# Top-k attention and Fourier mixing on one core: the scores of two query tiles in one burst of four matmuls, the second tile's fetched from the banks of the transposes one and two steps later

## The chip, the cores and the metric

The kernel runs on one core of a Trainium2 chip. The metric is the device time of one execution in microseconds (us). TensorE is called PE in the profile, VectorE DVE, ScalarE ACT, GpSimd POOL; SP issues DMAs.

## What is computed

```python
def _attn_ref(q, k, v):                      # (8, 8, 576, 64): batch, heads, tokens, head size
    scores = scale * np.matmul(q, k.transpose(0, 1, 3, 2))
    kth = np.partition(scores, -top_k, axis=-1)[..., -top_k:-top_k + 1]      # top_k = 32
    scores = np.where(scores >= kth, scores, -1000000000.0)
    attn = np.exp(scores - np.max(scores, axis=-1, keepdims=True))
    attn = attn / (np.sum(attn, axis=-1, keepdims=True) + 1e-09)
    return np.matmul(attn, v)
# attention's output as x (8, 576, 512), then
    X = np.fft.fft(np.fft.fft(x, axis=1), axis=2)
    u = x + np.real(X)
    un = (u - mean(u)) / np.sqrt(var(u) + 1e-06)
    return u + np.maximum(un @ w_ch1, 0.0) @ w_ch2      # 512 -> 2048 -> 512
```

All arithmetic is in 32-bit floats. The weights come as 64-bit floats and are converted in the first stage.

## The kernel before

Heads are worked on in pairs, four pairs to a batch and 32 in all. The 64 columns of one head lie on partitions 0 to 63 and those of the other on 64 to 127, so that the two heads' score matmuls use different halves of PE's rows. A pair's queries make five tiles: four of 128 rows, each of which gives two items (one per head), and one of 64 rows in which both heads lie together. In the order of `IN_PAIR` a pair has nine items: tile 0 (items 0 and 1), tile 1 (2, 3), the small tile 4 (item 4), tile 2 (5, 6), tile 3 (7, 8). There are 288 items, and one step of the main loop for each.

Everything is written out in one hand-made order. Step i does the following, each engine taking its instructions strictly in this order:

- PE computes scores for item j = i + 3. For an item with head 0 the function `scores` makes two matmuls of 128 x 512 (L401), one for each head, whose results ACT copies into the tiles `S` (L404). The last 64 keys, called the tails, come from a matmul of their own (`sp_t`, L371) and are copied by two short copies (L375). The small tile has its own form (L386, L393).
- DVE finds the 32 largest of 576 scores in four rounds of `max` (L425) and three of `match_replace` (L427): the last two rounds of item i and the first two of item i + 1.
- POOL then makes the two bounds `nt` (L434). In the next step ACT writes a mask into `wk` (L448), POOL subtracts it (L451), and ACT takes the exponential (L459).
- In most pairs (pairs 4, 5, 6 and 8 to 30: `by_dma`) the probabilities are transposed by DMA: ACT splits each 32-bit word into two planes (two copies, L472), SP writes them to DRAM (L485 and L488) and reads them back transposed (`turn`, L506) into `PT`. In the others PE transposes them (L527).
- PE multiplies `PT` by v (`o`, L564), ACT copies the result (`xT`, L578) and the sums (`rd`, L590), PE transposes it back to tokens (`tpx`, L604), and DVE normalises it into x (L608, L615).
- At steps 0 and 5 of a pair PE transposes the next q and k (`prep`, L308).

Beside the attention of one batch run the transforms and the two-layer network of an earlier one. The Fourier transform is folded on POOL (`fold_ops`, L651 to L719), multiplied on PE (`yp`, L755; `mp`, L812 and L816) and copied by ACT (`y`, L786 to L791; `us`, L833); POOL adds it to x (L839), DVE takes the statistics (L844). The network is cut into units: `hidden` (hp, L966, with ACT's copy hT, L970) and `back` (cp, L993 and L1032; the products cv and cw, L1163, with sums on POOL, L1108, copies on ACT, L1133, and loads of `w2` parts on SP, L909). A planner decides how many units a step takes: `fixed_cost` is its estimate of the step's other PE work, `level` the common height to which steps are filled, and `some` runs units after each piece of the step's PE list `fixed`. The list begins with the scores; work in `last_scores` is put at its end, and there stood the scores of a pair's tile 0.

PSUM has eight banks: two for scores (`ps_s`), two for the transposes of q, k and probabilities and, in `by_dma` pairs, for the tails (`ps_t`), one for o and tpx (`ps_o`), three for the units (`ps_m`). Buffers of a pool are handed out in turn; a matmul into a bank waits until ACT has read what was there before. `S` has six buffers, `W` (the tiles `wk`) three.

Of the kernel before, what the change touches and what calls it, by code (L numbers as in the profile page):

```python
# [9 lines left out]
F32 = mybir.dt.float32  # L10
# [9 lines left out]
P = 128  # L20
# [53 lines left out]
def kernel(  # L74
# [9 lines left out]
    nc = tc.nc  # L84
    B, H, S, D = q.shape
# [5 lines left out]
    NF = NC - 1  # L91
# [239 lines left out]
    items = [(pair, t, e) for pair in range(NPAIR) for t, e in IN_PAIR]  # L331
    N = len(items)

    def scores(i, part):


# [3 lines left out]
        pair, t, e = items[i]  # L340
        qT, kT = qT_of[pair], kT_of[pair]
        rows = ROWS[t]
        if part == 0:
            for n in range(1 if e is None else 2):
                Ssb[i + n] = attp.tile([P, S], F32, name=f"S_{i + n}", tag="S", bufs=6)
        q_cols = slice(P * t, P * t + rows)
# [91 lines left out]
    def pair_by_dma(pair):  # L438

        return NPB <= pair < NPAIR - 1 and pair != 2 * NPB - 1  # L440

    def by_dma(i):
        return pair_by_dma(i // PER_PAIR)
# [22 lines left out]
    def plane(i, half):  # L466

        if not (0 <= i < N and by_dma(i)):
            return
        words = Wk[i].bitcast(U16).rearrange("p (h s) -> p h s", h=2)  # L470
        src = Ssb[i].bitcast(U16).rearrange("p (s h) -> p h s", h=2)
        nc.scalar.copy(out=words[:, half, :], in_=src[:, half, :])  # L472
        if half == 0:
            return
        Ssb.pop(i)
        Wk.pop(i)
        pair, t, e = items[i]
        nq = TAIL if e is None else P
        if e != 1:
            planes_of[pair, t] = dramp.tile(  # L480
                [nq, 2, 2 * S], U16, name=f"planes_{pair}_{t}", tag="planes", bufs=3
            )
        to = planes_of[pair, t]
        if e is not None:
            nc.sync.dma_start(out=to[:, :, S * e:S * (e + 1)], in_=words)  # L485
        else:
            for h in range(2):
                nc.sync.dma_start(  # L488
                    out=to[:, :, S * h:S * (h + 1)], in_=words[nq * h:nq * (h + 1)]
                )  # L490
        if e != 1:
            Wp.pop(i)
# [965 lines left out]
    def fixed_cost(i):  # L1458

        t = 0.55 if 0 <= i - 2 < N and not by_dma(i - 2) else 0.0  # L1460
        if i + 3 < N:
            t += {0: 1.04, 1: 0.3, None: 0.9}[items[i + 3][2]]
            if by_dma(i + 3) and items[i + 3][2] is not None:
                t += -0.3 if items[i + 3][2] else 0.3
        ch = chunk_at(i)[1] if i > PER_BATCH + 3 else {4: 0, 8: 1}.get((i - 3) % PER_PAIR)
        t += 0.0 if ch is None else (CW[ch] / 115.0 + 0.14 * len(CHUNKS[ch]))
        if i < N and i % PER_PAIR in (0, 5):
            t += 0.7
        return t + costs.get(i, 0.0)
# [9 lines left out]
    def run(i, where):  # L1479
        for fn in plan.pop((i, where), []):  # L1480
            fn()
# [16 lines left out]
    while i < N + 5 or plan or queue or sums:  # L1498
# [18 lines left out]
        if i < N and i % PER_PAIR == 5:  # L1517
            preps.append(lambda: prep("k", pair_of + 1))
        last_scores = []
        if PER_BATCH < j < N and j % PER_PAIR == 0 and by_dma(j):  # L1520
            fixed.append(lambda: 0.0)
            last_scores.append(lambda: scores(j, 0) + scores(j, 1))
        elif e == 0 and by_dma(j):
            fixed.append(lambda: scores(j, 0) + scores(j, 1))
        elif e != 1:
            fixed.append(lambda: scores(j, 0))
        elif not by_dma(j):
            fixed.append(lambda: scores(j - 1, 1))
        else:
            fixed.append(lambda: 0.0)  # L1530
# [13 lines left out]
            fixed += tok  # L1544
        for where in ("pe1", "pe2", "pe"):
            fixed += plan.pop((i, where), [])
        if e is None and j < N:
            fixed.append(lambda: scores(j, 1))
        n_tr = len(fixed)
        if done is not None:  # L1550
# [19 lines left out]
            mask(i - 1)  # L1570
        plane(i - 2, 0)
        plane(i - 2, 1)
        run(i, "convert")
        if short:
            expo(i - 1)
# [98 lines left out]
```

## Time and profile before

| | |
|---|---|
| median of three runs | 1861.7 us (1857.86 to 1864.14) |
| profiled execution, its own time | 1856.28 us |
| span in the profile | 1854.5 us |
| mean granted PE clock | 0.96 |
| busy PE / DVE / ACT / POOL | 1688.5 / 1584.3 / 1294.3 / 912.5 us |
| score matmuls L401 | 528 records, 170.4 us busy |
| fetches of scores L404 | 264 copies, 588 ns mean |
| tails sp_t L371 | 320 records |

One matmul of 32-bit floats appears as two records, each with its own weight load (PEld). A row of the timeline merges equal instructions that follow each other: start, length of the merged run, engine, line, operation, tiles written and read, size, count, and in brackets the idle time before it and the instruction that ended it. The profile shows one execution, and durations are taken from there; so a sum is made against 1856.28 us.

### The profile page before, as it was taken

What the parts mean: (1) busy time and instruction counts of PE and PEld (TensorE: products, weight loads), DVE (VectorE), ACT (ScalarE), POOL (GpSimd) and SP (SyncE); (2) the same over time, 40 slices, a digit from 0 to 9 for tenths busy, and PEclk for the clock granted to TensorE, in tenths of its full rate; (3) what the DMA queues carried; (4) which work ended last, traced back from release to release, by engine and by line L of the source; (5) the groups of instructions that cost most, each with busy time, mean ns of one, the idle gap of its engine ahead of it and who ended that gap; (6) DMA issues with size and microseconds to landing.
All of it is one profiled execution on the core that took longest, in us unless ns stands there. A gap on an engine that the chain in (4) does not pass through costs nothing.

```text
span 1854.5 us, 26992 instructions
## 1 busy us (share of the span) xinstructions
PE 1688.5 (91%) x8134; PEld 1082.4 (58%) x8134; DVE 1584.3 (85%) x3301; ACT 1294.3 (70%) x3104; POOL 912.5 (49%) x1278
## 2 busy tenths in 40 slices
PE   5676699789899898999999999999999999999999
PEld 3343465355465664557565665667565756686677
DVE  7999989889999999999999999999999998944010
ACT  6878658577688778878788778877887778642100
POOL 4768743454753466346543565355634654350012
PEclk8778799899999999999999999999999999999999
DMA  5333115661456954568465945586457845520051
GB/s 168 106 88 114 27 41 148 186 168 38 121 137 158 233 151 123 134 178 222 112 153 146 246 124 137 141 222 171 122 137 180 213 112 140 153 82 7 6 173 57
DMA packets 516576, 249.16 MB, mean 134 GB/s; under 512 B 398288, under 2 KB 506448, under 8 KB 516432
## 3 DMA queue, kind: packets, MB, share of 16 engines
q1 hardware_dynamic: 515664, 247.23, 51.2%
q8 instruction: 65, 1.06, 0.2%
q14 instruction: 79, 0.65, 0.1%
q10 hardware_dynamic: 768, 0.21, 0.0%
HBM read 93.63 MB, written 84.74 MB: 96 GB/s over the span
## 4 chain that ended last, share of the span: by engine, by line
PE 43%; DVE 24%; POOL 11%; ACT 9%; issue 7%; DMA 4%; SPq 1%; POOLq 0%; DVEq 0%; ACTq 0%
PE hp L966 15%; DVE wk L427 11%; DVE m L425 10%; PE o L564 5%; PE cp L993 5%; POOL wk L451 5%; PE cw L1163 4%; PE sp L401 3%; ACT wk L448 2%; PE cv L1163 2%; POOL fg L651 2%; PE yp L755 2%; ACT wk L472 1%; POOL zw L678 1%; PE cp L1032 1%
## 5 line engine op out<-in xcount | busy, mean ns | idle before, releaser
L451 POOL TENSOR_TENSOR wk<-S,wk 128x576 f32<-128x576 f32 x288 | 407.5, 1415 | 485.2 <-ACT wk L448 484.8
L425 DVE MAX8 m<-wk 128x8 f32<-128x576 f32 x864 | 626.4, 749 | 6.1
L966 PE MATMUL hp<-unT,w 128*128 128x256 f32 (+1 forms) x2048 | 526.1, 409 | 5.3 <-ACT hT L970 4.6
L966 PEld LDWEIGHTS hp<-unT,w 128*128 128x128 f32 x2048 | 380.3, 191 | 109.8 <-issue 10.4
L427 DVE MATCH_REPLACE8 wk<-m,wk 128x576 f32<-128x576 f32 x576 | 427.5, 742 | 0.0
L472 ACT COPY wk<-S 128x576 uint16<-128x576 uint16 x468 | 289.6, 670 | 0.0
L448 ACT ACTIVATE wk<-S,nt 128x576 f32<-128x576 f32 x288 | 223.4, 776 | 85.3 <-POOL nt L434 84.0
L993 PE MATMUL cp<-w,hT 128*128 128x512 f32 x512 | 234.9, 599 | 0.0
L970 ACT ACTIVATE hT<-hp 128x320 f32<-128x320 f32 (+1 forms) x256 | 103.3, 411 | 177.2 <-PE hp L966 175.6
L425 DVE MAX8 m<-S 128x8 f32<-128x576 f32 x288 | 213.7, 742 | 15.6 <-ACT S L375 15.6
L459 ACT ACTIVATE S<-wk,nt 128x576 f32<-128x576 f32 x234 | 184.2, 787 | 50.5 <-POOL wk L451 49.2
L427 DVE MATCH_REPLACE8 wk<-m,S 128x576 f32<-128x576 f32 x288 | 213.7, 742 | 0.0
L564 PE MATMUL o<-PT,v 128*64 128x256 f32 (+3 forms) x1440 | 199.3, 421 | 14.5 <-ACT x L627 5.9
L401 PE MATMUL sp<-kT,qT 64*128 64x512 f32 (+1 forms) x528 | 170.4, 673 | 12.2 <-ACT means L1357 5.7
L564 PEld LDWEIGHTS o<-PT,v 128*64 128x64 f32 x1440 | 115.7, 155 | 90.8 <-issue 22.3
L404 ACT COPY S<-sp 128x512 f32<-128x512 f32 (+1 forms) x264 | 141.8, 588 | 27.9 <-PE sp L401 26.9
L993 PEld LDWEIGHTS cp<-w,hT 128*128 128x128 f32 x512 | 93.9, 192 | 90.2 <-issue 89.3
L1108 POOL TENSOR_TENSOR hT<-hT 128x512 f32<-128x512 f32 x64 | 81.2, 1275 | 117.0 <-ACT hT L970 87.9
L434 POOL TENSOR_TENSOR nt<-m,cc 128x2 f32<-128x2 f32 x288 | 60.2, 209 | 155.4 <-DVE m L425 154.8
L1163 PE MATMUL cw<-w,hT 128*128 128x256 f32 x448 | 105.3, 385 | 12.2 <-ACT ct L1133 10.1
L371 PEld LDWEIGHTS sp_t<-kt,qT 128*128 128x128 f32 x320 | 51.0, 194 | 108.9 <-issue 67.6
L1163 PEld LDWEIGHTS cw<-w,hT 128*128 128x128 f32 x448 | 83.1, 191 | 27.9 <-ACT ct L1133 12.5
(160 smaller groups left out, 2129.6 us busy)
## 6 DMA issues: line engine op xcount, KB each, us to landing
planes<-wk SPq DMA_DIRECT2D x208, 288.0 KB, 2.7
w<-w_parts SPq DMA_DIRECT2D x82, 512.0 KB, 4.7
space<-in_moe_w_ch_dram SPq DMA_DIRECT2D x32, 512.0 KB, 3.6
nat<-in_q_dram SPq DMA_DIRECT2D x128, 64.0 KB, 2.3
v<-in_v_dram SPq DMA_DIRECT2D x64, 128.0 KB, 2.9
out_dram<-x SPq DMA_DIRECT2D x32, 256.0 KB, 2.8
nat<-in_k_dram SPq DMA_DIRECT2D x62, 128.0 KB, 3.0
planes<-wk SPq DMA_DIRECT2D x52, 144.0 KB, 2.6
```

What stands on the lines that cost most here:

```text
L401: nc.tensor.matmul(sp[r], lhsT=qT[hd, q_cols], rhs=kT[hd, :], start=True, stop=True)
L404: nc.scalar.copy(out=s_t[r, keys], in_=sp[r])
L425: ops.append(lambda src=src, m8=m8: nc.vector.max(out=m8, in_=src))
L427: ops.append(lambda src=src, m8=m8: nc.vector.match_replace(w, m8, src, NEG))
L448: nc.scalar.activation(out=w, in_=Ssb[i], func=AF.Relu, scale=-FAR, bias=Nt[i][:, 1:2])
L451: nc.gpsimd.tensor_tensor(out=w, in0=Ssb[i], in1=w, op=ALU.subtract)
L459: nc.scalar.activation(out=Ssb[i] if by_dma(i) else w, in_=w, func=AF.Exp, bias=Nt.pop(i)[:, 0:1], accum_out=den_t[pair % 3][:, c:c + 1],)
L472: nc.scalar.copy(out=words[:, half, :], in_=src[:, half, :])
L564: nc.tensor.matmul(o[D * e:D * (e + 1), c0:c1], lhsT=vv[:, c, e, :], rhs=pt[:, NF if c == NF else (NF + 1) * e + c, c0:c1], start=(c == 0) ...
L966: nc.tensor.matmul(hp[:, 0:w], lhsT=w1[:, dt, P * it:P * (it + 1)], rhs=unT[:, dt, 0:w], start=(dt == 0), stop=(dt == NDT - 1),)
L993: nc.tensor.matmul(cp, lhsT=hT[:, it, P * n:P * (n + 1)], rhs=w2[:, it, :], start=(it == 0), stop=(it == NIT - 1),)
L1163: nc.tensor.matmul(dst, lhsT=h()[a][:, kc, :], rhs=rhs_of(kc), start=start and kc == 0, stop=kc == NK - 1, skip_group_check=True,)
```

## The change

In the pairs with transposes by DMA, the scores of two tiles of 128 rows are computed in one burst of four matmuls: tiles 0 and 1 at the end of the step that used to do tile 0 (only where the pair before is such a pair too), tiles 2 and 3 at the end of the step that used to do tile 2 at its beginning. The first tile's two results go to the score banks and are copied at once, as before. The second tile's two results go to the two banks of `ps_t` and stay there; ACT copies them with `fetch`, head 0 one step later, head 1 two steps later, behind the plane copies of that step. The tails keep their steps, and there they now stand alone: before the burst for tiles 0 and 2, at the usual place for tiles 1 and 3. The planner's estimates follow: 2.4 us in a burst step, 0.3 us in the second tile's step.

```diff
+    def in_burst(i):
+        if not (0 <= i < N and by_dma(i)):
+            return False
+        r = i % PER_PAIR
+        return r >= 5 or (r < 4 and pair_by_dma(i // PER_PAIR - 1))
+
+    held = {}
+
+    def burst(i):
+        pair, t, _ = items[i]
+        for n, pool, tag in ((0, ps_s, "sp"), (2, ps_t, "tp")):
+            t = items[i + n][1]
+            for h in range(2):
+                hd = slice(D * h, D * (h + 1))
+                sp = pool.tile([P, NF * P], F32, name=f"sp_{i + n}_{h}", tag=tag)
+                nc.tensor.matmul(
+                    sp, lhsT=qT_of[pair][hd, P * t:P * (t + 1)], rhs=kT_of[pair][hd, :],
+                    start=True, stop=True,
+                )
+                held[i + n + h] = sp
+        for h in range(2):
+            fetch(i + h)
+        return 2.1
+
+    def fetch(i):
+        if i not in held:
+            return
+        if i not in Ssb:
+            Ssb[i] = attp.tile([P, S], F32, name=f"S_{i}", tag="S", bufs=6)
+        keys = slice(TAIL, S) if items[i][2] else slice(0, NF * P)
+        nc.scalar.copy(out=Ssb[i][:, keys], in_=held.pop(i))
...
-            if by_dma(i + 3) and items[i + 3][2] is not None:
+            if in_burst(i + 3):
+                t = t - 1.04 + {0: 2.4, 5: 2.4, 2: 0.3, 7: 0.3}[(i + 3) % PER_PAIR] if items[i + 3][2] == 0 else t - 0.3
+            elif by_dma(i + 3) and items[i + 3][2] is not None:
                 t += -0.3 if items[i + 3][2] else 0.3
...
-        if PER_BATCH < j < N and j % PER_PAIR == 0 and by_dma(j):
+        if in_burst(j) and e == 0:
+            fixed.append(lambda: scores(j, 1) if j % PER_PAIR else 0.0)
+            if j % PER_PAIR in (0, 5):
+                last_scores.append(lambda: burst(j))
+        elif PER_BATCH < j < N and j % PER_PAIR == 0 and by_dma(j):
             fixed.append(lambda: 0.0)
             last_scores.append(lambda: scores(j, 0) + scores(j, 1))
...
-        if e is None and j < N:
+        if j < N and (e is None or in_burst(j) and j % PER_PAIR == 0):
             fixed.append(lambda: scores(j, 1))
...
         plane(i - 2, 0)
         plane(i - 2, 1)
+        if j % PER_PAIR in (1, 2, 6, 7):
+            fetch(j + 1)
         run(i, "convert")
```

More of the change, by code (lines that the diff above doesn't have):

```diff
@@ L342, in scores @@
         rows = ROWS[t]
-        if part == 0:
+        if part == 0 or in_burst(i) and i not in Ssb:
             for n in range(1 if e is None else 2):
```

## Prediction

> **What bounds the kernel now.** I read the page first: part 1 and the chain of part 4.
>
> ```profile
> PE 1688.5 (91%) x8134; PEld 1082.4 (58%) x8134; DVE 1584.3 (85%) x3301; ACT 1294.3 (70%) x3104; POOL 912.5 (49%) x1278
> PE 43%; DVE 24%; POOL 11%; ACT 9%; issue 7%; DMA 4%; SPq 1%; POOLq 0%; DVEq 0%; ACTq 0%
> ```
>
> These are averages over stages, so I cut the span with the windows view (columns: stretch, length, busy time and instructions of PE, PEld, DVE, ACT, POOL, granted clock, DMA share, GB/s).
>
> ```profile
> 460.00:1560.00 1100.00, 1054.28 (x5174) 667.09 (x5172) 1056.49 (x2194) 867.83 (x2064) 587.60 (x872) 0.99 0.63 159
> 1560.00:1660.00 100.00, 98.83 (x488) 68.15 (x487) 75.77 (x158) 59.65 (x145) 39.01 (x48) 1.00 0.46 126
> ```
>
> Up to 1560 us DVE and PE are both 96% busy. In slices without a wait DVE shows 19.7 of 20 us, so 98.7% is its ceiling and PE follows it closely. From 1560 us PE alone is the bound, into the tail. The batches repeat every 200.5 us (the wait at 902 us comes again at 1103, 1303 and 1504). In the middle stage only work that makes DVE wait costs time, and these waits are few. The timeline of DVE (start, us, instruction, idle time before it and its releaser):
>
> ```profile
> 1045.13 0.09 DVE L427 MATCH_VALUE_LOAD wk<-m,S 128x8 f32 x1 [1.52 <-DMA w<-w_parts]
> 1066.25 0.42 DVE L608 TENSOR_TENSOR x<-tpx,rd 128x256 f32<-128x256 f32 x1 [1.39 <-PE tpx L604]
> 1102.98 0.19 DVE L591 RECIPROCAL rd<-rd 128x6 f32<-128x6 f32 x1 [0.84 <-ACT rd L590]
> 1131.58 0.76 DVE L425 MAX8 m<-S 128x8 f32<-128x576 f32 x1 [2.23 <-ACT S L375]
> 1137.30 0.69 DVE L844 BATCH_NORM_STATS2 st<-x 128x6 f32<-128x512 f32 x1 [0.32 <-POOL x L839]
> 1575.88 0.43 DVE L608 TENSOR_TENSOR x<-tpx,rd 128x256 f32<-128x256 f32 x1 [3.31 <-PE tpx L604]
> ```
>
> The first five are one batch's waits, 6.3 us in all; the last begins the stage where PE is late.
>
> **What a burst saves on PE.** The timeline of PE shows a tile's two score matmuls (four records) with the tails after them, and tails that stand alone between other work:
>
> ```profile
> 709.84 1.13 PE L401 MATMUL sp<-kT,qT 64*128 64x512 f32 x4
> 710.90 0.49 PE L371 MATMUL sp_t<-kt,qT 128*128 128x128 f32 x2
> 711.23 5.32 PE L993 MATMUL cp<-w,hT 128*128 128x512 f32 x12
> ...
> 796.68 0.39 PE L371 MATMUL sp_t<-kt,qT 128*128 128x128 f32 x2
> 796.90 2.32 PE L966 MATMUL hp<-unT,w 128*128 128x320 f32 x8
> ```
>
> From start to start the pair takes 1.06 us, tails behind it 0.33, tails alone 0.22. A record of 512 columns at 128 rows takes 5.32/12 = 0.443 us, so four in a row would be 1.77: the two heads, in different row halves, overlap, and a pair is 2 x 0.443 = 0.89 of streaming and 0.17 of entering the half-row shape. A burst of two tiles is then 4 x 0.443 + 0.17 = 1.94 against 2.12, a saving of 0.18. Two tails of 0.33 become two of 0.22, and the matmul behind the burst pays that 0.11 once: 0.11 more. Sum 0.29 us. Bounds: only the 0.11, if the second pair doesn't overlap with the first; 0.35 + 0.22 = 0.57, if the whole fixed part vanishes. I take 0.29, since the pair already shows almost perfect overlap. There are 26 pairs of heads on the DMA path; all have the second burst, 24 the first: 50 bursts, 14.5 us of PE (5.5 to 28). Most of it is hidden, as DVE is the bound.
>
> The Trainium skill speaks against such packing (TensorEngine Tiling, Performance Considerations): tiling speeds up the matmuls, not the emptying of PSUM, which can become the limit. By it the four copies of a burst, 0.588 us each on the page, would pace it at 2.35 us, and nothing would be saved. The rows above show PE going on from a pair without waiting for its copies, and here the second tile's copies are put off; what that costs is the next part.
>
> **What it adds: waits for banks.** The pool of the transposes has two banks, taken in turn. Before, only tails and transposes of q and k use it here. Now in each burst step the order of requests is tails, third matmul, fourth matmul, so the fourth takes the bank that the same step's tails have just filled, and PE stops there until ACT has copied these tails (L375). ACT does that behind the step's mask and two plane copies. The order listing of the changed program has an ACT wait on each of these fourth matmuls. How long? By today's lag between PE's scores and ACT's fetch of them, first PE's timeline, then ACT's:
>
> ```profile
> 1101.13 1.89 PE L401 MATMUL sp<-kT,qT 64*128 64x512 f32 x4 [0.43 <-ACT S L393]
> 1127.32 1.13 PE L401 MATMUL sp<-kT,qT 64*128 64x512 f32 x4
> 1175.36 1.13 PE L401 MATMUL sp<-kT,qT 64*128 64x512 f32 x4
> ```
> ```profile
> 1106.12 1.07 ACT L404 COPY S<-sp 128x512 f32<-128x512 f32 x2
> 1130.30 1.06 ACT L404 COPY S<-sp 128x512 f32<-128x512 f32 x2
> 1176.52 1.07 ACT L404 COPY S<-sp 128x512 f32<-128x512 f32 x2 [0.62 <-PE sp L401]
> ```
>
> For a pair's first burst the tails stand right before it: PE is ready for the fourth matmul 0.25 + 1.3 = 1.55 us after the place where L401 starts now, and the bank is free 0.4 us after ACT's place. At 1127 that is 1130.7 - 1128.9 = 1.8 us of waiting; at 1023, 1075 and 1175, where ACT waits for PE, none. For the second burst one unit (1.75) lies between: at 1101 (tails from 1100.5) it is 1106.5 - 1103.8 = 2.7, at 1150 likewise 2.6, and at 998 and 1050, where the lag is 2.2 and 2.0 us, none. So three of eight bursts wait, 7.1 us per batch, where POOL's folds (L651, L678) hold ACT up. Removed are the stalls of the second burst's tile behind L393 (0.75 at 1101, 0.5 at 1150). Net on PE per batch: +7.1 - 1.3 - 8 x 0.29 = +3.5 us. It is covered as long as PE has idle time later: 0.39 at 1020, 1.68 at 1030, 1.78 at 1060, together 3.85 per batch. In the last batch that cover is gone. There I follow the row of 1150: its burst ends at 1155.4 + 0.9 = 1156.3, and with two cp units (3.5), o (2.3), tails (0.2) and one hp (2.15) PE is at its second hp unit at 1164.5, where it now is at 1161.25: **3.2 us late**, which the PE-bound end keeps.
>
> The early fetches of the second tile, 0.59 us each (L404), stand on ACT behind the planes and before the Exp, one in each of the two steps after a burst. ACT's count doesn't change and it is 79% busy in the middle stage, but what is queued behind comes later: hT and us copies, y copies. One has no slack: us (L833) - POOL's add (L839) - DVE's statistics at 1137 (0.32 late already). I take 0.5 us per batch, four batches: +2.0 (0 to 0.6 each).
>
> Tails (sp_t) of the second tile, and the transposes of q and k behind them, need a bank that a fetch of the step before frees. The transposes wait for that copying today (3.71 us longest, L308); I leave it at nothing (between 0.6 less and 0.5 more each, by one copy).
>
> **What moves earlier.** The second burst goes from the start of its step to its end, behind the step's transposes of x (tpx), and the pair of the tile after next leaves the start of its own step. So tpx comes 1.06 + 0.33 - 0.22 = 1.16 us sooner there. DVE's waits for tpx at 462 and 513 (2.73, 1.64) shrink by 1.16 each, -2.3; those at 1066, 1266, 1467 (1.39, 0.68, 1.64) by 1.16, 0.68, 1.16, -3.0. The wait for rd (0.84, four times) loses perhaps 0.2 each, -0.8, as PE's run before it has 1.4 us less to do and DVE comes 1.2 earlier.
>
> Moving the units moves their DMAs on SP: the loads of w2 parts (512 KB) now stand one behind, not two in front of, the planes that free the work buffer which DVE waits for at 1045 (also 1.64 at 1246, 1.44 at 1445). One load less at the 263 GB/s of 1030 to 1062 us is 2.0 us. Taken at 0.6 of 4.6 us: -2.8 (0 to -4.6). S itself is fetched a step earlier for two tiles in four; only the wait at 1131 could gain, and its 0.3 us is in the 0.5 above.
>
> **Sum.** DVE's stages: -2.3 - 3.0 - 2.8 - 0.8 + 2.0 = -6.9. PE at the end: +3.2. Together -3.7 us against the profiled execution: 1856.3 (1854.5 of span, 1.8 around it) to 1852.6. Its median is 1861.7, so I name 1858.0. A measurement of this kernel tells about 0.3%, 5.6 us, from no change.
>
> **Rivals.** (1) Slower: the fourth matmul's wait becomes the bound. For: PE has only 46 us of idle time in 1100, and Exp and fetches queue behind a burst that waits, so ACT's lag feeds itself. Against: today's 3.85 us per batch of idle time. If none of it absorbs, 5.5 batches x 3.5 = 19, less the 6.9: +12, 1874. It decides as soon as a batch waits more than 3.85 + 2.3 us in bursts: the three at 7.1, or five at 1.3. (2) Clearly faster: the waits are shorter than today's lag says, since PE no longer runs ahead, and the last batch loses nothing: -6.9, the four 0.5 back, and the waits from 1575 to 1635 (3.3, 2.3) reduced by 4 bursts x 0.29 and 1.0 at one tpx: about -11, 1851. (3) The second pair doesn't overlap: 9 us of PE less saved, 0.7 of it in the last batch; -3.0, which can't be told from the forecast and gets no chance of its own.
>
> **Numbers.** Forecast 0.43, of which 0.11 beyond -0.3% and 0.32 within; its own range is 1850 to 1864. Rival 1 0.35, rival 2 0.22. So faster 0.33, same 0.32, slower 0.35. The range takes in both rivals' prices and leaves their far ends out: 1844 to 1876.
>
> **What would show it.** Right: L401 in runs of eight records, 1.9 to 2.0 us where nothing waits; three bursts per batch stretched by 2 to 3 us, released by ACT S; L608 at 1066 without a wait; the batch period 200 us or a little less; PE some 3 us later than DVE at 1575. Wrong: stretched bursts in the hp stages too, PE idle up and DVE waiting for tpx in the middle stage, a period over 201 (rival 1); hardly any stretched burst (rival 2); eight records in 2.1 us or more without a wait (rival 3).

## The result, and the profile after

The changed kernel takes 1886.35 us in the median of four runs (1883.09 to 1889.77), the kernel before 1860.98 beside it (1857.86 to 1864.14): a ratio of 1.0136 [1.0111, 1.0162], 25 us slower. The prediction said 1858.0, 1844 to 1876. The profiled executions are 30.5 us apart (spans 1854.5 and 1885.0); the readings below belong to these two.

The page of the changed kernel, part 1 and the chain of part 4:

```profile
PE 1707.9 (91%) x8134; PEld 1100.0 (58%) x8134; DVE 1581.8 (84%) x3301; ACT 1304.0 (69%) x3104; POOL 911.2 (48%) x1278
PE 51%; POOL 13%; ACT 12%; DVE 12%; issue 7%; DMA 3%; SPq 1%; POOLq 0%; DVEq 0%
```

PE was to become less busy; it is 19 us more busy, and its share of the chain that ends last grew from 43% to 51%, while DVE's halved. The order of events says where the time goes. DVE's wait for rd at 459.03 us comes 2.4 us earlier than before, the one at 511.13 is 1.4 later, the one at 902.45 is 9.3 later, at 1102.98 17.1, at 1302.91 25.5, at 1503.60 26.7, and the end 30.5. So the stages up to 902 us lose 9 us, the next two batches 8 each, the batch after them 1, the end 4.

The timeline of DVE (start, us, instruction, idle time before it and its releaser) in the batch shown before:

```profile
1067.35 0.42 DVE L643 TENSOR_TENSOR x<-tpx,rd 128x256 f32<-128x256 f32 x1 [1.29 <-PE tpx L639]
1080.06 0.42 DVE L643 TENSOR_TENSOR x<-tpx,rd 128x256 f32<-128x256 f32 x1 [1.44 <-PE tpx L639]
1120.06 0.19 DVE L626 RECIPROCAL rd<-rd 128x6 f32<-128x6 f32 x1 [4.11 <-ACT rd L625]
1151.86 0.76 DVE L460 MAX8 m<-S 128x8 f32<-128x576 f32 x1 [5.56 <-ACT S L367]
1157.32 0.69 DVE L879 BATCH_NORM_STATS2 st<-x 128x6 f32<-128x512 f32 x1 [1.08 <-POOL x L874]
...
1608.29 0.43 DVE L643 TENSOR_TENSOR x<-tpx,rd 128x256 f32<-128x256 f32 x1 [3.16 <-PE tpx L639]
```

The wait for the W buffer (1.52 at 1045) is gone, as forecast. In its place the wait for rd has gone from 0.84 to 4.11 us and that for S from 2.23 to 5.56, and there is a second tpx wait. From 440 to 1640 us of the kernel before, and over the same work (440 to 1668 us) of the changed one, DVE's waits over 0.25 us add up to 43.0 and 74.4 us: rd 6.4 to 17.8, S 8.9 to 21.9, statistics 1.3 to 7.1, tpx 19.8 to 26.2, W 4.9 to 0. Of the 26.2 us, 6.5 end with the DMA that writes the old x out; before there were none of these. The 31 us more are about the whole lag gained there (from 2.4 us early to 28.1 late). DVE does the same work; it waits for ACT and POOL, which wait for PE.

PE's timeline in the same batch shows the bursts (L351), the tails (L406) and what follows:

```profile
1089.36 1.98 PE L351 MATMUL sp<-kT,qT 64*128 64x512 f32 x6
1092.20 1.12 PE L351 MATMUL sp<-kT,qT 64*128 64x512 f32 x2 [0.86 <-ACT S L410]
...
1119.66 2.00 PE L351 MATMUL sp<-kT,qT 64*128 64x512 f32 x6
1123.57 1.39 PE L351 MATMUL sp<-kT,qT 64*128 64x512 f32 x2 [1.92 <-ACT S L410]
1124.89 2.93 PE L1028 MATMUL cp<-w,hT 128*128 128x512 f32 x3
...
1149.58 2.86 PE L351 MATMUL sp<-kT,qT 64*128 64x512 f32 x8
...
1172.87 1.98 PE L351 MATMUL sp<-kT,qT 64*128 64x512 f32 x6
1176.20 1.12 PE L351 MATMUL sp<-kT,qT 64*128 64x512 f32 x2 [1.35 <-ACT S L410]
```

A burst breaks after six of its eight records: the fourth matmul (two records) waits for ACT's copy of the tails. The bracket shows only what is left after the modelled end of the row in front, so I read how far a burst is stretched from first start to last end, against 2.0 us of an undisturbed one: 1.96, 3.3, 0.86 and 2.45, 8.6 us in this batch; 6.6 in the next (1297 to 1382 us). A stretch is not all idle time. The burst at 1149 shows none: single records of its third matmul start at 1150.54 and 1150.97, of its fourth at 1151.32 and 1151.85, where an undisturbed burst (781 us) starts them in pairs 0.01 us apart. So a fourth matmul that comes late also takes from the third the partner beside which it runs.

The three cp records at 1124.89 take 2.93 us, where four usually take 1.88. The windows view says why (the third column from the end is the granted clock):

```profile
1122.00:1124.00 2.00, 0.43 (x1) 0.29 (x2) 2.00 (x5) 1.98 (x7) 1.89 (x2) 1.00 1.16 255
1124.00:1128.00 4.00, 4.00 (x6) 1.42 (x5) 3.93 (x10) 3.10 (x7) 3.11 (x4) 0.57 0.24 78
```

During the stall the clock is still 1.00, behind it 0.57 for 4 us, which by estimate (4 x 0.43) costs another 1.7. Between 440 and 1640 us twelve bursts are stretched by 2 us or more, and after nine of them the clock falls to 0.50 for some 3 us or longer; after the twelve stretched by 0.3 to 1.4 us it never does. By the clock records of the traces (time at half clock, halved) this takes 10 us of full speed from PE before and 27 after, over the same work as above. The cp and hp records, the same matmuls in both kernels, take 17 us more (cp 234.9 to 241.9, hp 526.1 to 535.8).

The three batches between the waits for rd at 902, 1103, 1303 and 1504 us (times of the kernel before) show what goes together:

| batch | bursts stretched by (stretches over 0.2 us) | falls of the clock behind bursts | time lost |
|---|---|---|---|
| 902 to 1103 | 6.8 us | 2 | 7.8 us |
| 1103 to 1303 | 8.6 us | 2 | 8.4 us |
| 1303 to 1504 | 4.9 us | 0 | 1.2 us |

How PE's lateness reaches DVE is seen in front of the S wait at 1151. ACT's and POOL's timelines of the changed kernel, and behind each the row of the kernel before for one of its rows:

```profile
1139.61 0.69 ACT L1055 ACTIVATE hT<-cp,gi 128x512 f32<-128x512 f32 x1 [3.69 <-PE cp L1028]
1143.44 0.77 ACT L483 ACTIVATE wk<-S,nt 128x576 f32<-128x576 f32 x1 [3.14 <-POOL nt L469]
1150.95 0.32 ACT L410 COPY S<-sp_t 128x64 f32<-128x64 f32 x2
1151.15 1.09 ACT L367 COPY S<-sp 128x512 f32<-128x512 f32 x2
...
1122.80 0.78 ACT L448 ACTIVATE wk<-S,nt 128x576 f32<-128x576 f32 x1 [3.14 <-POOL nt L434]
```
```profile
1140.38 1.27 POOL L1057 TENSOR_TENSOR x<-x,hT 128x512 f32<-128x512 f32 x1 [6.19 <-ACT hT L1055]
1141.61 1.40 POOL L686 TENSOR_TENSOR fg<-zw 128x254 f32<-128x254 f32 x2
1143.22 0.19 POOL L469 TENSOR_TENSOR nt<-m,cc 128x2 f32<-128x2 f32 x1
...
1119.74 1.27 POOL L1022 TENSOR_TENSOR x<-x,hT 128x512 f32<-128x512 f32 x1 [2.62 <-ACT hT L1020]
```

The cp unit behind a stalled burst is late; ACT waits 3.69 us for it, POOL's add behind that 6.19 (2.62 in the kernel before), the folds and the bound nt come behind the add, the mask behind nt, and tails and fetch behind the mask, at 1151. The mask's own wait for nt, 3.14 us, is as long as before; all of it only comes later. MAX8 then waits 5.56 - 2.23 = 3.3 us longer than before, and POOL's add 3.6. PE's few late microseconds travel through three queues and end in DVE.

### The profile page after: what moved, and what is told of

Same layout as the page of the kernel before. It is cut to its first block, busy times and chain, and to the rows that moved or that the text cites. A ratio compares the mean times of both kernels' runs of the same rounds, so it can differ in the third digit from the quotient of the medians.

```text
span 1885.0 us, 26974 instructions
## 1 busy us (share of the span) xinstructions
PE 1707.9 (91%) x8134; PEld 1100.0 (58%) x8134; DVE 1581.8 (84%) x3301; ACT 1304.0 (69%) x3104; POOL 911.2 (48%) x1278
## 4 chain that ended last, share of the span: by engine, by line
PE 51%; POOL 13%; ACT 12%; DVE 12%; issue 7%; DMA 3%; SPq 1%; POOLq 0%; DVEq 0%
PE hp L1001 20%; PE o L599 6%; DVE m L460 6%; DVE wk L462 5%; PE cp L1028 5%; POOL wk L486 5%; PE cw L1198 4%; ACT wk L483 3%; PE cv L1198 3%; PE sp L351 3%; POOL fg L686 3%; ACT wk L507 2%; PE cp L1067 2%; ACT S L494 1%; POOL sd L754 1%
## 5 line engine op out<-in xcount | busy, mean ns | idle before, releaser
L1001 PE MATMUL hp<-unT,w 128*128 128x256 f32 (+1 forms) x2048 | 535.8, 414 | 7.9 <-ACT hT L1005 4.6
L1001 PEld LDWEIGHTS hp<-unT,w 128*128 128x128 f32 x2048 | 385.1, 193 | 131.3 <-issue 23.0
L1028 PE MATMUL cp<-w,hT 128*128 128x512 f32 x512 | 241.9, 613 | 0.0
L351 PE MATMUL sp<-kT,qT 64*128 64x512 f32 x400 | 128.4, 631 | 23.2 <-ACT S L410 23.2
L367 ACT COPY S<-sp 128x512 f32<-128x512 f32 x200 | 112.8, 593 | 23.0 <-PE sp L351 19.8
L1198 PE MATMUL cv<-w,hT 128*128 128x256 f32 x384 | 94.5, 393 | 7.1 <-DMA w<-w_parts 4.1
L1198 PEld LDWEIGHTS cw<-w,hT 128*128 128x128 f32 x448 | 83.4, 191 | 25.5 <-ACT ct L1168 8.0
```

The lines of the kernel that those rows point to most:

```text
L351: nc.tensor.matmul(sp, lhsT=qT_of[pair][hd, P * t:P * (t + 1)], rhs=kT_of[pair][hd, :], start=True, stop=True,)
L367: nc.scalar.copy(out=Ssb[i][:, keys], in_=held.pop(i))
L1001: nc.tensor.matmul(hp[:, 0:w], lhsT=w1[:, dt, P * it:P * (it + 1)], rhs=unT[:, dt, 0:w], start=(dt == 0), stop=(dt == NDT - 1),)
L1028: nc.tensor.matmul(cp, lhsT=hT[:, it, P * n:P * (n + 1)], rhs=w2[:, it, :], start=(it == 0), stop=(it == NIT - 1),)
L1198: nc.tensor.matmul(dst, lhsT=h()[a][:, kc, :], rhs=rhs_of(kc), start=start and kc == 0, stop=kc == NK - 1, skip_group_check=True,)
```

## Experiments

Every ratio is against runs of the kernel before on the same chip, with its 95% interval. Two terms: "new prices" are the planner's estimates of the changed kernel, "old prices" those of the kernel before.

**1. The fourth matmul's wait, taken away.** In burst steps the tails go to a unit's bank:

```diff
-            if by_dma(i):
+            if in_burst(i) and i % PER_PAIR in (0, 5):
+                sp = bank(shape, name)
+            elif by_dma(i):
                 sp = ps_t.tile(shape, F32, name=name, tag="tp")
```

> The tails of a burst step go to one of the three banks of the units instead of one of the two banks of the transposes, so the fourth matmul of a burst has a free bank and waits for no copy of this step; the order of instructions on PE is that of the changed kernel. Theory A (the fourth matmul's wait for the bank is what costs): the stalls in front of it (25 us between 520 and 1620 us in the changed kernel's trace, 4 to 5 per batch) vanish and with them the 25 us of the result: 1856 to 1866 us. Theory B (the units of PE stand in other places now, so that a cp unit ends later and POOL's folds, the masks and the fetches behind it come late): the time stays at 1880 to 1890. Theory C (the second tile's fetches stand in front of Exp on ACT and make ACT late): likewise 1880 to 1890. If the stall only moves to a unit that waits for its bank: 1875 or more, with idle time in front of cp, hp or tpx.

Measured: 1868.36 us, 1.0047 [1.0032, 1.0062]. Two thirds of the loss are gone, but not all: theory A holds for 16 of the 25 us, and 9 are left. No burst waits now (PE's timeline):

```profile
1110.25 2.00 PE L351 MATMUL sp<-kT,qT 64*128 64x512 f32 x8
1112.18 5.42 PE L1030 MATMUL cp<-w,hT 128*128 128x512 f32 x12
```

From start to the next start a burst takes 1.93 us. The batch period is back at 200.8 and 200.5 us (S waits at 938.06, 1138.87, 1339.39), and the clock is 1.00 from 760 to 1360. But waiting has moved as well: the tails now find the unit's bank not yet read. PE's groups (line, shapes, busy us and mean ns, idle time before and its releasers) of the changed kernel and of this run:

```profile
L406 PE MATMUL sp_t<-kt,qT 128*128 128x128 f32 x320 | 67.8, 301 | 17.2 <-ACT S L439 8.3 <-ACT qT L316 6.3 <-ACT S L428 1.7
...
L408 PE MATMUL sp_t<-kt,qT 128*128 128x128 f32 x320 | 71.4, 310 | 39.6 <-ACT S L441 8.8 <-ACT unT L921 8.7 <-ACT y L828 8.5
```

That is 22 us more in front of the tails for 23 less in the bursts, and yet 16 us of time are won. So PE's idle time alone does not tell what a wait costs, and the 9 us left may be these waits or something else.

**2. The burst undone, its order and prices kept.** The second pair of matmuls goes back to its own step and to the score banks:

```diff
-        for n, pool, tag in ((0, ps_s, "sp"), (2, ps_t, "tp")):
...
+        for h in range(2):
+            hd = slice(D * h, D * (h + 1))
+            sp = ps_s.tile([P, NF * P], F32, name=f"sp_{i}_{h}", tag="sp")
...
-            fixed.append(lambda: scores(j, 1) if j % PER_PAIR else 0.0)
+            fixed.append(lambda: (j % PER_PAIR in (2, 7) and burst(j), scores(j, 1))[1] if j % PER_PAIR else 0.0)
```

> The first tile's pair stays at the end of the burst step, but the second tile's pair goes back to the start of its own step, into the banks of the scores, and is fetched at once; the planner's prices and so the places of the units are those of the changed kernel. No bank of the transposes holds scores. Theory A (bank wait): 1857 to 1866 us, nearly the time before. Theory B (places of the units, and the second burst at the step's end): 1880 to 1890. Theory C (early fetches in front of Exp): 1857 to 1866 like A.

Measured: 1871.45 us, 1.0070 [1.0050, 1.0090]. It lies between the theories: with no scores in the banks of the transposes at all, half of the loss stays. So part of the loss is not in the banks.

**3. The banks held longer.** The second tile's fetches stand behind Exp instead of in front of it:

```diff
...
-        if j % PER_PAIR in (1, 2, 6, 7):
-            fetch(j + 1)
...
                 expo(i - 1)
+                if j % PER_PAIR in (1, 2, 6, 7):
+                    fetch(j + 1)
```

> The second tile's fetches are moved on ACT from in front of Exp to behind it, in the same steps; everything else is the changed kernel. Theory C (fetches in front of Exp make ACT late): 1866 to 1876 us, a large part of the loss back. Theory A: the banks are freed later, so the tails and transposes behind wait longer: 1886 to 1892. Theory B: no change, 1883 to 1889.

Measured: 1905.22 us, 1.0256 [1.0216, 1.0297]. Theory C is out: early fetches don't hurt, late ones cost 22 us more. The sign is theory A's, the size far beyond its 6 us: the banks come free one Exp later (0.8 us and 0.2 for its sum). The wait is where theory A puts it, in front of the tails and the transposes, not in the bursts: in PE's groups idle time before the tails grows from 17.2 to 26.7 us and before tpq from 8.7 to 25.2, while that before the bursts falls from 23.2 to 16.8.

**4. Only the first burst.**

```diff
-        return r >= 5 or (r < 4 and pair_by_dma(i // PER_PAIR - 1))
+        return r < 4 and pair_by_dma(i // PER_PAIR - 1)
```

> Only the first burst of a pair of heads is made (24 of 50); the second one's tiles are scored as before, each in its own step. Theory A: both kinds of burst stall, so about half of the loss, 1870 to 1876 us. Theory B, since the step of the second burst then starts with its scores again and the units behind it stand nearly as before: 1858 to 1866. Theory C: half of the fetches are gone, 1870 to 1876 like A.

Measured: 1869.68 us, 1.0060 [1.0043, 1.0077]: just under half of the loss, at the edge of theory A's figure.

**5. The prices alone.** The kernel before, with the changed kernel's `fixed_cost` and the same sums returned by `scores`; no burst, no fetch put off:

```diff
-            if by_dma(i + 3) and items[i + 3][2] is not None:
+            if in_burst(i + 3):
+                t = t - 1.04 + {0: 2.4, 5: 2.4, 2: 0.3, 7: 0.3}[(i + 3) % PER_PAIR] if items[i + 3][2] == 0 else t - 0.3
+            elif by_dma(i + 3) and items[i + 3][2] is not None:
...
-            last_scores.append(lambda: scores(j, 0) + scores(j, 1))
+            last_scores.append(lambda: scores(j, 0) + scores(j, 1) + (1.06 if in_burst(j) else 0.0))
...
-            fixed.append(lambda: scores(j, 0) + scores(j, 1))
+            fixed.append(lambda: scores(j, 0) + scores(j, 1) + ((1.06 if j % PER_PAIR == 5 else -1.04) if in_burst(j) else 0.0))
```

> The kernel before with nothing but the changed kernel's prices in the planner, so that PE's units stand in the steps where the changed kernel has them; there are no bursts, no early fetches and no scores in the banks of the transposes, and the second pair of tiles of a pair of heads is scored at the start of its step. Theory B1 (what is left of the loss without the bank wait, about 10 us, comes from the units' places): 1866 to 1872 us, with PE waiting about 4 us for POOL's folds near 480 us and the granted clock at 0.50 after that. Theory B2 (it comes from the second burst at the end of its step): 1856 to 1862, no different from the kernel before.

Measured: 1869.13 us, 1.0053 [1.0035, 1.0071]. Theory B1 holds: the places of the units alone cost 10 us, on a kernel without a burst. PE's timeline, here first of the kernel before and then of this one, and the windows of this one show the expected place:

```profile
474.06 3.60 PE L993 MATMUL cp<-w,hT 128*128 128x512 f32 x8
479.36 0.46 PE L755 MATMUL yp<-fs,fg 128*64 128x145 f32 x2 [1.70 <-POOL fg L651]
...
475.01 1.88 PE L1000 MATMUL cp<-w,hT 128*128 128x512 f32 x4
480.82 0.74 PE L762 MATMUL yp<-fs,fg 128*64 128x145 f32 x2 [3.92 <-POOL fg L658]
```
```profile
477.00:481.00 4.00, 0.18 (x1) 0.19 (x2) 3.97 (x8) 3.17 (x8) 3.55 (x6) 0.77 0.30 87
481.00:484.00 3.00, 2.47 (x18) 1.97 (x19) 2.93 (x6) 0.04 (x1) 2.93 (x10) 0.50 0.58 148
```

In the kernel before, eight cp records (3.60 us) stand in front of the transform's first matmul, which then waits 1.70 us for POOL's folds, at a clock of 1.00. With the new prices four records stand there, the wait is 3.92, and the transform runs at half clock. This is one place of several. Most of the cost lies ahead of 902 us: DVE's wait for rd at 511 comes 2.1 us later than in the kernel before, that at 902 9.1, that at 1504 11.6. DVE's timeline shows two larger waits, where the kernel before has none for tpx and 0.61 us for POOL:

```profile
633.61 0.42 DVE L615 TENSOR_TENSOR x<-tpx,rd 128x256 f32<-128x256 f32 x1 [3.07 <-PE tpx L611]
862.46 0.48 DVE L1128 SCALAR_TENSOR_TENSOR x<-cv,gi,x 128x256 f32<-128x256 f32 x1 [2.48 <-POOL x L1142]
```

Which unit makes which wait was not tried. And this kernel with the new prices, against experiment 1 with the same prices, gives the bursts' own worth: PE 1690.4 us busy against 1677.2, 13 us less, and the time is the same (1.0053 and 1.0047), with the tails' new waits of experiment 1 in it.

**6. The bursts with the old prices.** First the change with the old prices and nothing else:

```diff
-            if in_burst(i + 3):
-                t = t - 1.04 + {0: 2.4, 5: 2.4, 2: 0.3, 7: 0.3}[(i + 3) % PER_PAIR] if items[i + 3][2] == 0 else t - 0.3
-            elif by_dma(i + 3) and items[i + 3][2] is not None:
+            if by_dma(i + 3) and items[i + 3][2] is not None:
...
-        return 2.1
+        return 1.04
...
-            fixed.append(lambda: scores(j, 1) if j % PER_PAIR else 0.0)
+            fixed.append(lambda: scores(j, 1) + (0.0 if j % PER_PAIR == 5 else 1.04) if j % PER_PAIR else 0.0)
```

> The changed kernel with only the planner's prices of the kernel before: bursts, banks and fetches are those of the change, and nearly every unit of PE stands in its old step. The prices alone cost 10 us on the kernel before (1869.1 against 1858.8). Theory D (the two costs add up: 10 us of places, 15 us of bank waits): 1872 to 1878 us. Theory E (the bank wait costs what the places leave open, so that the old places bring nothing or less): 1882 to 1892. Theory F (the bank wait is harmless with the old places): 1858 to 1864.

Measured: 1.0090 [1.0064, 1.0117] (1881.87 us; the kernel before took 1865.62 on this chip, so this is 1875.6 against the 1858.8 of the expectation). Theory D: the two parts add up, in sum. Places cost 0.53% without bursts and 1.0136 - 1.0090 = 0.46% with them; bursts 0.83% to 0.90%, under either prices. By place they do not add so neatly: with the old prices, too, DVE's wait for rd at 902 comes late, by 13.6 us, where the places should cost nothing any more.

Then old prices and the tails in a unit's bank (the edits of experiments 1 and 6 together):

> Both bursts and the early fetches, the tails of a burst step in a bank of the units (so no wait of the fourth matmul), and the planner's prices of the kernel before, so that nearly every unit stands in its old step. Theory B1 (units' places): the loss is gone, 1850 to 1860 us. Theory B2 (second burst at the end of its step): 1866 to 1870.

Measured: 1868.69 us, 1.0053 [1.0032, 1.0074]; the figure of theory B2. Whether for its reason this run can't say, since the tails wait for the unit's bank here too, and longer than in experiment 1 (43.1 us in front of them for 39.6; again at 1157.83, 1.74 us for ACT's unT). PE's timeline:

```profile
1131.66 0.80 PE L408 MATMUL sp_t<-kt,qT 128*128 128x128 f32 x2 [2.98 <-ACT y L828]
```

The old prices do take away the loss ahead of 902 us (rd comes 0.1 us late there, 7.4 in experiment 1); the loss is now in the batches (11.3 us late at 1504).

**7. Three more with the tails in a unit's bank.** New prices, the second burst in front of its tails at the start of its step:

> As with the tails in a bank of the units, and the second burst stands at the start of its step, in front of its tails, where the kernel before scores that tile; planner's prices of the changed kernel. Theory B1: 1866 to 1871 us, as with the tails in a unit bank alone (1868.4). Theory B2: 1852 to 1860.

Measured: 1869.63 us, 1.0061 [1.0041, 1.0082], as theory B1 says: with the new prices the burst's place in its step brings nothing. New prices, first burst only:

> Only the first burst of a pair of heads, with its tails in a bank of the units. With the bank wait it took 1869.7 us, 11 us over the kernel before. Theory A for that loss (bank wait): 1856 to 1862 us. Theory B1 (prices of the first burst's two steps): 1865 to 1870.

Measured: 1863.35 us, 1.0022 [1.0011, 1.0033]; just above theory A's figure, against 1.0060 with the bank wait. The same with old prices:

> Only the first burst, its tails in a bank of the units, the planner's prices of the kernel before. With the new prices the same took 1.0022 of the kernel before. If the units' places were the rest of that loss: 0.996 to 1.000. If bursts cost by what they hold (two banks of the transposes for one to two steps, fetches in front of Exp): 1.002 to 1.004.

Measured: 1865.06 us, 1.0034 [1.0021, 1.0047]: no gain from the old prices here, and the figure of the second guess, that bursts cost by what they hold. Old prices, both bursts, the second at the start of its step:

> Both bursts, tails in a bank of the units, old prices, and the second burst at the start of its step, in front of its tails. With that burst at the end of its step the tails waited 3.0 us per batch for a unit's bank behind the y copies, and the time was 1.0053 of the kernel before. If that wait and the late copies of S were the loss: 0.995 to 1.001. If bursts cost by what they hold: 1.004 to 1.007.

Measured: 1862.32 us, 1.0019 [1.0007, 1.0031], the best form with bursts. Between the two expected figures: 22 of the 25 us are undone, and nothing is won, though PE is 3 us less busy than before. Against the second burst at the end of its step, with the same prices, 0.34% is gained; the edit moves the burst and shortens the tails' waits (43.1 to 29.0 us) in one, so theory B2 and these waits are not told apart. This form also shows what a batch absorbs: between 902 and 1504 us two bursts of each batch are stretched, by 1.43 and 1.89 us, the clock stays at 1.00, and DVE's wait for rd is 2.0 us late at the start and 1.1 at the end. Here 3.3 us of stretch per batch, with the bursts' saving on PE against them, cost nothing.

**8. The tails in an empty quarter of a bank.** o and tpx use 384 of the 512 columns of their bank, and tails need 128; so the tails of all `by_dma` tiles were put into the last quarter. The control has this alone, on the kernel before:

```diff
+    o_bank = ps_o.tile([P, 4 * P], F32, name="o_bank", tag="o")
...
-                sp = ps_t.tile(shape, F32, name=name, tag="tp")
+                sp = o_bank[:, 3 * P:4 * P]
```

> The control for the run before it: the kernel before with its tails in the last quarter of the bank of o, no bursts. Removes the wait of the transposes of q and k for the tails' copies (10 us in front of them in the trace of before, nearly all of it ahead of 760 us); adds 18 waits for DVE. 1852 to 1864 us; if the 18 waits count, up to 1868.

> Old prices as in the run before, and the tails (128 columns) of all tiles on the DMA path lie in the last quarter of the bank of o and tpx, so that the banks of the transposes hold only second tiles and transposes of q and k; no fourth matmul waits for a copy and no tail waits for a unit's bank (18 of the 147 tails wait for a normalisation on DVE instead). Theory D (both costs gone): 1850 to 1860 us, PE 13 us less busy. If the second burst at the end of its step or the early fetches cost something by themselves: 1864 to 1870, as with the tails in a unit bank and old prices (1868.7).

Measured: 1.0128 [1.0104, 1.0152] for the control, 1.0225 [1.0208, 1.0243] with the bursts. Both miss. PE's groups in the control show a new wait:

```profile
L373 PE MATMUL o_bank<-kt,qT 128*128 128x128 f32 x260 | 65.4, 335 | 38.2 <-ACT xT L580 35.9 <-ACT S L377 1.9
```

The tails wait for ACT's copy of o, which lies in other columns. In the run with bursts the same group waits 49.3 us, 13.3 of them for copies of S, so the 0.97% between the two can't be put down to the bursts as such. The Trainium skill (PSUM — Partial Sum Buffer, PSUM bank collisions raise a hardware error) states that the compiler's scheduler makes any two instructions of different engines wait for each other if they touch the same bank and the same 32 partitions, whatever the columns; these 35.9 us agree with it. But the tails and o are slices of one tile here (`o_bank`), so that this run can't tell a wait for the bank from a wait for the tile.

**9. The copy of the tails, moved on ACT.** In burst steps plane copies and tails stand in front of the mask, so that ACT copies the tails while it would wait for POOL's bound:

```diff
...
+        early = in_burst(j) and j % PER_PAIR in (0, 5)
+        if early:
+            plane(i - 2, 0)
+            plane(i - 2, 1)
+            scores(j, 1)
         if by_dma(i - 1):
             mask(i - 1)
-        plane(i - 2, 0)
-        plane(i - 2, 1)
+        if not early:
+            plane(i - 2, 0)
+            plane(i - 2, 1)
```

> In a burst step the plane copies and then the tails stand at the start of the step, in front of the mask that waits for POOL, so that ACT copies the tails while it would wait for that mask's bound; the fourth matmul still takes the bank of these tails. All else as in the changed kernel, its prices too. Theory G (the wait is made by the copy's place in ACT's order): the stalled bursts are gone, and what remains is the 10 us of the units' places: 1.004 to 1.007 of the kernel before, 1866 to 1872 us. Theory H (the mask, now behind planes and tails, comes late and with it POOL, Exp and the planes of the next step): 1.012 or more, 1882 us and up.

> The same order on ACT with the planner's prices of the kernel before, so that nearly every unit of PE stands in its old step. Theory G: both parts of the loss are gone, 0.996 to 1.002 of the kernel before, 1853 to 1865 us. Theory H: 1.006 to 1.012, as with the old prices alone (1.009).

> As the run before it, but only the first burst of a pair of heads; the second tile pair is scored as in the kernel before. Theory G: half of the work that PE saves (6 us), hidden in the middle: 0.996 to 1.001 of the kernel before. Theory H: 1.003 to 1.006.

> Only the second burst, at the end of its step, with tails and planes in front of the mask and the old prices. Theory G: 0.996 to 1.001. If the second burst's move from the start of its step to the end costs something by itself (the first copies of S then come later, and DVE waits for them): 1.004 to 1.008, with MAX8 waiting for S.

Measured, in this order: 1.0108 [1.0080, 1.0137], 1.0052 [1.0033, 1.0072], 1.0028 [1.0013, 1.0043], 1.0053 [1.0032, 1.0073]. None lies in theory G's range. The first three lie between the two theories; the last has the figure of its rival (the second burst's move to the end), but not its sign, since MAX8 waits for S 2.2 to 2.3 us per batch, as in the kernel before. Theory G is half right: the stalls shrink. Idle time in front of L351 falls from 23.2 us to 10.7 with the new prices and from 25.5 to 15.8 with the old ones, the burst at 1149 and its like run in 1.99 us, and the first two versions are 0.3% and 0.4% under their sisters (1.0136, 1.0090), with intervals that overlap. But other bursts still wait 1.40 us, and the tails, now earlier on PE, wait for ACT's copy of kt (both rows with the old prices):

```profile
1111.64 1.12 PE L351 MATMUL sp<-kT,qT 64*128 64x512 f32 x2 [1.40 <-ACT S L410]
...
1132.54 0.49 PE L406 MATMUL sp_t<-kt,qT 128*128 128x128 f32 x2 [2.58 <-ACT kt L322]
```

Here too the old prices are worth 0.56%.

## Why the prediction was wrong, step by step

**What a burst saves: right.** Predicted 1.94 us from start to start, measured 1.92 and 1.93 where nothing waits; for the whole kernel 14.5 us of PE predicted, 13 measured (experiments 1 and 5). The pace of the copies, of which the Trainium skill (TensorEngine Tiling, Performance Considerations) warns as a possible limit (2.35 us a burst), does not show: four copies at 0.592 us each would be 2.37. "Most of it is hidden" was too weak: all of it is.

**The fourth matmul's wait: right in sum, in part by luck.** Predicted 7.1 us per batch, measured 8.6 and 6.6 of stretch. The places differed, and two misses nearly cancel: one burst of an hp stage is stretched by 1.96 us where nothing was expected, and the first burst near 1149 by 0.86 for 1.8. The text counted waiting alone; part of each stretch is the third matmul running without its partner.

**The cover: this step failed.** The text took the net 3.5 us per batch for hidden, since PE has 3.85 us of idle time later in the batch. The batches lost 7.8, 8.4 and 1.2 us. What it put at nothing is what follows a stall. The clock fell behind two bursts of each of the two dear batches, by estimate 1.7 us each, and behind none of the cheap one, whose bursts were still stretched by 4.9 us. And the delay does not stay on PE, where idle time could take it up: from a late cp it goes through ACT and POOL to the masks and copies of S, as shown at 1139 to 1151. The order of events is against the cover, too: outside the bursts PE has no idle time of 0.5 us between 1072 and 1244 us, and DVE has already waited for rd at 1120 and for S at 1151. Of the gaps that were counted, the largest is there as before, first in the kernel before, then in the changed one (PE's timeline):

```profile
1029.94 3.72 PE L1163 MATMUL cw<-w,hT 128*128 128x256 f32 x16 [1.68 <-ACT ct L1133]
...
1047.20 1.99 PE L1198 MATMUL cw<-w,hT 128*128 128x256 f32 x8 [1.75 <-ACT ct L1168]
```

It ends with ACT's copy of PE's own cw result, which ACT takes in its order, behind a mask, two plane copies, a fetch and Exp; so here its end is set by ACT's order and not by when PE gets there. Only the 1.78 us in front of o (a wait for a DMA) went. Some cover there is: the best form of experiment 7 absorbs 3.3 us per batch. That the clock makes the difference is likely, but was not tried by itself.

This was rival 1, with its condition (waits above 3.85 + 2.3) met; its price of 12 us was too small for the same reasons. In the runs the bursts' part is 0.83% to 0.90%, 15 to 17 us, and with the fourth matmul's wait gone it is nothing under the new prices.

**The places of the units: a term that the sum lacks.** Of the units that the new prices move, the text costed one tpx and the loads of w2. It never asked what stands in front of the transform's first matmul afterwards, though the row at 479.36 (1.70 us for POOL) was in the trace. Experiment 5 prices all the moved units at 10 us, most of it ahead of 902 us and with the sign against the forecast.

**What moves earlier.** The W wait went, by 4.9 us for the 2.8 forecast. tpx, forecast 5.3 us better, is 6.4 worse in sum (19.8 to 26.2): what waits for PE is unchanged (462 is gone, but 1080 is new), and 6.5 us for the DMA that writes x out came to it, which the text did not have. rd, forecast 0.8 better, is 11.4 worse; it stands on ACT behind the y copies, which wait for PE in both kernels (2.81 us at 1095 before, 1.94 at 1112 after), so that PE's lateness reaches it. The path from us to the statistics, put at 2.0, cost 5.8.

**The end: about right.** Forecast 3.2 us of PE, measured 30.5 - 26.7 = 3.8 between 1503 us of before and the end. The bursts there are four with 0.25 to 1.33 us of stretch, 3.2 us together, and not the one path that the text followed, so the figure owes something to luck. Waits of tails and transposes for second tiles, put at nothing: sp_t went from 13.6 to 17.2 us of idle time, tpq and tpk from 20.7 to 13.7 together.

So the forecast of -3.7 us missed 15 to 17 us of bank waits that were found, sized and wrongly called covered, and 10 us of units' places that were not looked for. The two add up to the measured 25; the gains on tpx and rd that were to outweigh them did not come.

**Left open.** The clock's share was not tried by itself. It is no measure of time alone: the kernel with old prices and tails in a unit's bank loses as much clock between 460 and 1560 us as the changed one (25.6 us each, 8.5 before) and is 0.8% faster. The last 0.2% of the best form has no cause shown; it still waits at a few bursts (0.78 us at 1154). The old prices bring 0.4% to 0.6% in four pairs of kernels and nothing in the two others with tails in a unit's bank (both bursts with the second at the end of its step, and the first burst alone); for the first of these the loss has moved into the batches, where the tails wait, and that these waits are its cause is argued only. That bursts cost by what they hold was met by one run (1.0034) and missed by the next (1.0019).

## What to carry to other kernels

Before idle time is counted as cover for a new wait, look at what comes first: the gap, or the next wait of the engine that sets the time; and at what ends the gap, which may be another engine's order. Count what follows a stall as well, here a lower clock and matmuls that lose their partner. A bank that a result waits in costs what is queued for the ring behind it, and in a ring of two the next request but one is often in the same step; price it by the place of the releasing copy in the other engine's order, and look at what that copy stands behind. When a change comes with new estimates for a planner, run the estimates alone on the old kernel.

## What the runs showed of the hardware

- The granted clock falls after short stalls. In the changed kernel bursts stretched by 2.0 us and more were followed by 0.50 in nine cases of twelve. The shortest three (881, 1089 and 1297 us) are stretched by 2.0 us, of which the profile shows 0.86 to 0.87 as idle; 3.0 us at 704 and 2.45 us at 1172 and 1377 were not followed by it. The trace's clock records change on a grid of 3.41 us, and the place on it matters: counted from the sixth record of a burst to the seventh, the nine waits have 1.38 us or more within one cell, at whose end the clock falls; those at 1172 and 1377 lie across a line, with at most 1.24 us on one side; 704, with 1.65, is an exception. The Trainium skill (TensorE: Matmul & The Clock Gate, Why this matters for your kernels) asks for no gaps above about 3 us; here 2 us were enough at times, and less by the profile's idle time. Its statement in Part 1 that the window of activity runs freely fits the grid.
- Two half-row pairs of 64x512 in a row take 1.93 us, four times 0.443 and 0.16: the fixed part is paid once per run of such matmuls, not once per pair. A pair whose second matmul comes late is stretched without any idle time (0.86 us at 1149).
- In this program a matmul into one quarter of a bank waits for ACT's copy out of other columns of it: 35.9 us in front of 130 tails (260 records). Both lie in one tile there, so whether the wait belongs to the bank or to the tile is not shown.
